# Two attention-and-MLP layers, one token, one core: the last wo loaded behind the last V, and the second layer's next K begun in quarters of chunks

## Chip, core and metric

The kernel runs on one core of a Trainium2 chip. The metric is device time in microseconds, the median of a few runs. Three runs of the kernel before gave 684.42 us (682.33 to 685.11).

## The reference

One token of width 512 goes through attention, MLP, attention, MLP; both attention blocks use the same weights and the same K and V caches, both MLPs the same weights. All of it is float32.

```
def _A_ref(x, k_cache, v_cache, wq, wo):              # 32 heads of 128, 4096 keys
    q = (x @ wq) as heads
    scores = einsum("bhqd,bhkd->bhqk", q, k_cache) * (Dh ** -0.5)
    p = softmax(scores)
    o = einsum("bhqk,bhkd->bhqd", p, v_cache)
    return o @ wo                                     # wq 512x4096, wo 4096x512
def _B_ref(x, w1, b1, w2, b2):                        # width 1376
    return gelu(x @ w1 + b1) @ w2 + b2

x = x + _A_ref(layernorm(x), ...)
x = x + _B_ref(layernorm(x), ...)
x = x + _A_ref(layernorm(x), ...)
x = x + _B_ref(layernorm(x), ...)
```

## The kernel before

**Work.** The 32 heads are taken in eight groups `g` of four. K and V of a group are 8 MiB each (128 partitions by 16384 floats); a group also needs 1 MiB of wq and 1 MiB of wo. K and V come in eight chunks `c` of 1 MiB (NC = 4U columns, U = 512), and a chunk has four quarters of U columns, one for each head. For each group PE computes the queries, the scores against eight chunks of K (`scores`, result in PSUM tile pS), DVE and ACT the softmax (`exponentials`, `weights`), PE the weighted sum of V (`values`, result in pO) and the product with wo (`head_out`). The first layer goes through g = 0 to 7, the second through g = 7 to 0, so that what is still in SBUF at the change of layers is used again.

**Storage.** All large operands live in one SBUF tile, `arena`, cut up by hand. In units of U columns: A is 0 to 32, C 32 to 64, B 64 to 96, of which the last 6 are also the first 6 of SHARED (90 to 100); SCRATCH is 100 (the softmax numerators, and pieces of `head_out` and of the MLP), PAIR is 101 to 109. K and V take A, B and C in turn. `load` (L68) issues one DMA on SyncE's queue (SP). A DMA that overwrites columns must wait until the DMAs that wrote them have landed and the engines that read them are done, and only for the columns that really overlap. SP issues its DMAs strictly in the order in which they are written: one that waits holds up all behind it. PE's matmuls are in the written order too (L74); DVE, ACT and GpSimd are ordered by the framework.

**End of the first layer (L314 to L342).** For g = 7 K is loaded into C in two halves, then wo into PAIR (L321), then V into A in four pieces (L322, 4, 2, 1 and 1 chunks). After the V loop come w1 in four rows (L331, L333) and w2 in four pieces (`load_w2`, called from inside `mlp`), which overwrite one another and SCRATCH in SHARED: the last row of w1 waits for SCRATCH, which `head_out` reads last at L225, and each piece of w2 for the rows of w1 under it.

**Start of the second layer (L346 to L383).** K and V of g = 7 are still in C and A. Of group 6's V 26 quarters were kept in B; six more went to spare PSUM banks (L328) and are copied back by ACT (L375). Group 6's K is loaded anew, by `begin_k`: chunk 0 to SHARED + 4U (over w2 rows 4 to 7), chunk 1 to PAIR + 4U (over the wq used just before), chunks 2 and 3 to C once the scores of g = 7 have read chunk 1 there, chunks 4 to 7 behind them once chunk 5 is read. Then `pair` goes to C + 24U: the wq of the following group (the first 4U) and the wo of group 6 (the other 4U). The two groups are computed from that; `next_queries(2, ...)` at L383 is the last reader of that wq. With n = 2 (group 5) the regular loop begins: K into A, then V into C in two pieces, ((0, 6), (6, 8)), that is C + 0 to 24U and C + 24U to 32U, then the next pair into PAIR, then the next K into B.

**End of the second layer.** As the first, but w1 and w2 go to A, which is free by then (L397 to L400).

Of the kernel before, what the change touches and what calls it, by code (L numbers as in the profile page):

```python
# [28 lines left out]
U = 512  # L29
NC = 4 * U  # L30
# [6 lines left out]
A_AT, B_AT, C_AT = RING  # L37
KEPT_V = 26 * U
SHARED = B_AT + KEPT_V
SCRATCH = SHARED + 10 * U  # L40
PAIR = SHARED + 11 * U
# [9 lines left out]
def decode_layers(ctx: ExitStack, tc: tile.TileContext, x, k, v, w, w1, b1, w2, b2, out):  # L51
    nc = tc.nc
# [4 lines left out]
    def ctile(name, *shape):  # L57
        return const.tile([P, *shape], F32, name=name)
# [6 lines left out]
    def at(first, n):  # L65
        return arena[:, first : first + n]

    def load(first, src):  # L68
        t = at(first, src.shape[-1])
        tc.keep_in_program_order(nc.sync.dma_start(t, src))  # L70
        return t

    def matmul(*a, **kw):
        tc.keep_in_program_order(nc.tensor.matmul(*a, **kw))  # L74

    def quarters(first):
        return [at(first + U * j, U) for j in range(4)]

    def part(src, g, a, b):
        return src[g][:, NC * a : NC * b]  # L80

    def of_w(row, i, n):
        return w[row][:, NC * i : NC * (i + n)]

    def by_four(t):
        return t.rearrange("p (j n) -> p j n", j=4)
# [12 lines left out]
    nc.vector.memset(negmean, -1.0 / D)  # L99
    power = ctile("power", 1)  # L100
    nc.gpsimd.memset(power, -0.5)


    pS, pO = (psum.tile([P, 512], F32, name=n) for n in ("pS", "pO"))
# [34 lines left out]
    def set_x(xin0, scale, xin1, queries=True):  # L139
        s = small("x_sum")  # L140
        t = x_wide if queries else small("x1", 8)
        if not queries:
            nc.gpsimd.memset(pairs(t)[:, :, 1], 1.0)
        x = pairs(t)[:, :, 0]
        nc.vector.scalar_tensor_tensor(x, xin0, scale, xin1, op0=ALU.mult, op1=ALU.add, accum_out=s)  # L145
        if queries:
            for j in range(1, J):
                nc.gpsimd.tensor_copy(pairs(t[:, 32 * j :])[:, :, 0], x)
        return t, s
# [34 lines left out]
    def scores(z, c, kt):  # L184
        for j in range(J):
            matmul(pS[32 * j : 32 * j + C, :], z[:, j, C - 1 - c : 2 * C - 1 - c], kt[j],
                   start=(c == 0), stop=(c == C - 1))

    def exponentials(sc, nsc):
        nc.vector.tensor_reduce(ml[:, 0:1], pS, axis=AX.X, op=ALU.max)  # L190
        mt, m, bias = small("mt", 32), small("m"), small("mt", 32)
        nc.vector.transpose(mt, ml)
        nc.vector.tensor_reduce(m, mt[:, :C], axis=AX.X, op=ALU.max)
        nc.vector.tensor_scalar(mb[:, :C], m.to_broadcast([P, C]), nsc, None, op0=ALU.mult)  # L194
        nc.vector.transpose(bias, mb)  # L195
        p = at(SCRATCH, U)
        nc.scalar.activation(p, pS, AF.Exp, bias=bias[:, 0:1], scale=sc, accum_out=ml[:, 0:1])  # L197
        return p

    def weights(p):  # L200
        for b in range(4):
            tc.keep_in_program_order(nc.tensor.transpose(  # L202
                pT[:, b].rearrange("p j r -> p (j r)"), p[:, P * b : P * (b + 1)], ident))
        pt = work.tile([P, P], F32, name="turned").rearrange("p (j c b) -> p j c b", j=J, c=C)
        nc.vector.tensor_copy(pt, pT[:, :, :, :C].rearrange("p b j c -> p j c b"))  # L205
        lt, l, lr, rl = small("mt", 32), small("l"), small("mt", 32), small("rl")
        nc.vector.transpose(lt, ml)  # L207
        nc.vector.tensor_reduce(l, lt[:, :C], axis=AX.X, op=ALU.add)
        nc.vector.tensor_copy(lb, l.to_broadcast([P, 32]))
        nc.vector.transpose(lr, lb)  # L210
        nc.vector.reciprocal(rl, lr[:, 0:1])
        return pt, rl

    def values(i, pt, vt, c):
        for j in range(J):
            matmul(pO[32 * j : 32 * j + 4, :], pt[:, j, c, :], vt[j],
                   start=(i == 0), stop=(i == C - 1))
# [52 lines left out]
    def load_w1(first, a, b):  # L270
        load(first + W1C * a, w1[:, W1C * a : W1C * b])

    def load_w2(first, a, b):
        load(first + U * a, w2[:, U * a : U * b])
# [4 lines left out]
    def blocks(src, g, home, pieces=((0, C),)):  # L279
        for a, b in pieces:  # L280
            load(home + NC * a, part(src, g, a, b))
            for c in range(a, b):
                yield c, quarters(home + NC * c)

    zero = ctile("zero", 4)
    nc.vector.memset(zero, 0.0)
    xs, s = set_x(zero, 1.0, xcol)

    def first_queries(xs, s, wt):
        for c in range(4):  # L290
            query_block(c, xs, wt)
            if c == 1:
                negm, ss = mean_of(xs, s)
        z = queries(0, negm)
        r = rstd_of(ss)
        sc, nsc = small("sc"), small("nsc")
        nc.vector.tensor_scalar(sc, r, DH ** -0.5, None, op0=ALU.mult)
        nc.vector.tensor_scalar(nsc, r, -(DH ** -0.5), None, op0=ALU.mult)
        return negm, z, sc, nsc
# [6 lines left out]
    def add_up(acc, own):  # L306
        t = small("acc", 4)
        nc.vector.scalar_tensor_tensor(t, own, 1.0, acc, op0=ALU.mult, op1=ALU.add)
        return t


    negm, z, sc, nsc = first_queries(xs, s, wq_t)
    acc = pairs(xs)[:, :, 0]
    for g in range(G):  # L314
        final = g == G - 1
        k_home, v_home = RING[2 * g % 3], RING[(2 * g + 1) % 3]
        for c, t in blocks(k, g, k_home, HALVES if final else ((0, C),)):
            scores(z, c, t)
        pt, rl = weights(exponentials(sc, nsc))
        if final:  # L320
            wo_t = by_four(load(PAIR, of_w(g % 2, g, 1)))  # L321
        for c, t in blocks(v, g, v_home, LAST if final else ((0, C),)):  # L322
            values(c, pt, t, c)
            if g == G - 2:
                for j in range(J):
                    i = 4 * c + j - KEPT_V // U
                    if i >= 0:
                        nc.scalar.copy(pK[i], t[j])  # L328
        if final:
            for i in range(3):  # L330
                load_w1(SHARED, i, i + 1)  # L331
            own = head_out(rl, wo_t, last=True)
            load_w1(SHARED, 3, 4)  # L333
        else:
            pair = load(PAIR, of_w(g % 2, g, 2))
            acc = add_up(acc, head_out(rl, by_four(pair[:, :NC])))
            wq_t = by_four(pair[:, NC:])
            z = next_queries(g + 1, xs, negm, wq_t)
# [4 lines left out]

    g = G - 2  # L346
    negm, z, sc, nsc = first_queries(xs, s, wq_t)
    acc = pairs(xs)[:, :, 0]
    wq_t = by_four(load(SHARED, of_w((g + 1) % 2, g, 1)))
    k_t = []  # L350

    def begin_k(home, a, b):
        load(home, part(k, g, a, b))
        k_t.extend(quarters(home + NC * i) for i in range(b - a))

    begin_k(SHARED + NC, 0, 1)
    begin_k(PAIR + NC, 1, 2)
    for c in range(C):
        scores(z, c, quarters(C_AT + NC * c))
        if c == 1:  # L360
            begin_k(C_AT, 2, 4)
        if c == 5:
            begin_k(C_AT + 2 * NC, 4, 8)
    pair = load(C_AT + 6 * NC, of_w(g % 2, g - 1, 2))
    p = exponentials(sc, nsc)
    z = next_queries(1, xs, negm, wq_t)
    pt, rl = weights(p)
# [2 lines left out]
    acc = add_up(acc, head_out(rl, wo_t))  # L370

    v_t = [at(B_AT + U * i, U) for i in range(KEPT_V // U)]
    for i, first in enumerate([SHARED + 8 * U, SHARED + 9 * U] + [PAIR + U * j for j in range(4)]):
        t = at(first, U)
        nc.scalar.copy(t, pK[i])  # L375
        v_t.append(t)
    for c in range(C):
        scores(z, c, k_t[c])
    pt, rl = weights(exponentials(sc, nsc))
    for c in range(C):  # L380
        values(c, pt, v_t[4 * c : 4 * c + 4], c)
# [1 line left out]
    z = next_queries(2, xs, negm, by_four(pair[:, :NC]))  # L383

    homes = (A_AT, C_AT, B_AT)
    for n in range(2, G):
        g, final = G - 1 - n, n == G - 1
        k_home, v_home = homes[(2 * n - 1) % 3], homes[2 * n % 3]
        for c, t in blocks(k, g, k_home, HALVES if final else ((0, C),)):
            scores(z, c, t)  # L390
        pt, rl = weights(exponentials(sc, nsc))
        if final:
            wo_t = by_four(load(PAIR, of_w(g % 2, g, 1)))
        for c, t in blocks(v, g, v_home, LAST if final else ((0, 6), (6, 8)) if n == 2 else ((0, C),)):
            values(c, pt, t, c)
        if final:
            for a, b in HALVES_W1:  # L397
                load_w1(A_AT, a, b)
            for a, b in W2_AT_END:
                load_w2(A_AT + 11 * U, a, b)  # L400
            own = head_out(rl, wo_t, last=True)
        else:
            pair = load(PAIR, of_w(g % 2, g - 1, 2))
            acc = add_up(acc, head_out(rl, by_four(pair[:, NC:])))
            z = next_queries(n + 1, xs, negm, by_four(pair[:, :NC]))
# [47 lines left out]
```

## Time and profile before

| | |
|---|---|
| median of three runs | 684.42 us (682.33 to 685.11) |
| the profiled execution | 684.1 us, its span 681.9 us, mean granted TensorE clock 0.841 |
| read from HBM | 286.14 MB, 420 GB/s over the span |
| busy: PE, DVE, ACT | 417.0 us (61%), 110.1 us (16%), 22.2 us (3%) |
| who was waited for on PE | DMA in_v 90.3 us, DMA in_k 66.2 us |

The span is the time from the first to the last instruction; the rest of the execution's time lies around it. Positions in the text are microseconds from the span's start. In the rows of the trace, "SPq L70 DMA_DIRECT2D arena<-in_k" is SP issuing a load of K at that moment; when it lands is a separate number, the time to landing.

### The profile page before, as it was taken

The numbers are of one execution on the slowest core, as the hardware profiler recorded it, in microseconds if no ns is written. First come the engines' busy times: TensorE is split into PE (matmuls) and PEld (weight loads), VectorE is DVE, ScalarE is ACT, GpSimd is POOL, SyncE is SP. The second block draws the span as 40 slices with busy tenths as digits, with TensorE's granted clock in tenths as the row PEclk, the third lists the DMA queues.
The fourth block names the chain that finished last, engine by engine and source line by source line (L and its number), as shares of the span: only waits on it lengthen the run. The fifth ranks groups of instructions, "written<-read, shape, count | busy, mean of one in ns | idle before, by whom it ended". The sixth has DMA issues, their size and how long they took to land. (4 is left out here: it accounts for less than half of the span.)

```text
span 681.9 us, 6303 instructions
## 1 busy us (share of the span) xinstructions
PE 417.0 (61%) x2768; PEld 115.8 (17%) x2768; DVE 110.1 (16%) x431; ACT 22.2 (3%) x47; POOL 4.3 (1%) x21
## 2 busy tenths in 40 slices
PE   1536566485564875547656897776456765656755
PEld 0102111021121211112103221221121111211212
DVE  1012101111011111211202212221021101210202
ACT  0010000000000000001000010000000000000000
POOL 1000000000000000000000000000000000000000
PEclk9969878797687876988976898989597876987968
DMA  9999999999999999999999999999999999999996
GB/s 369 432 431 431 439 442 451 432 433 431 428 431 405 454 428 431 431 417 433 430 405 319 354 451 425 399 446 428 443 435 415 455 431 428 431 443 409 428 414 273
DMA packets 10971, 286.54 MB, mean 420 GB/s; under 512 B 1728, under 2 KB 1728, under 8 KB 3008
## 3 DMA queue, kind: packets, MB, share of 16 engines
q1 hardware_dynamic: 10512, 286.14, 98.3%
q8 instruction: 21, 0.34, 0.2%
q10 hardware_dynamic: 432, 0.01, 0.0%
q14 instruction: 6, 0.05, 0.0%
HBM read 286.14 MB, written 0.00 MB: 420 GB/s over the span
## 5 line engine op out<-in xcount | busy, mean ns | idle before, releaser
L74 PE MATMUL pO<-arena,turned 128*4 128x512 f32 x1024 | 143.6, 722 | 91.6 <-DMA arena<-in_v 90.3
L74 PE MATMUL pS<-arena,zq 128*8 128x512 f32 x1024 | 135.1, 687 | 71.9 <-DMA arena<-in_k 66.2
L74 PE MATMUL pO<-arena,x_wide 128*128 128x512 f32 (+1 forms) x176 | 55.7, 533 | 25.1 <-DVE turned L134 18.1
L74 PE MATMUL pO<-arena,on_wide 128*128 128x512 f32 x112 | 51.8, 605 | 18.6 <-DVE on_wide L229 18.6
L74 PEld LDWEIGHTS pO<-arena,turned 128*4 128x4 f32 x1024 | 27.9, 97 | 197.0 <-issue 189.0
L74 PEld LDWEIGHTS pS<-arena,zq 128*8 128x8 f32 x1024 | 28.9, 98 | 174.9 <-issue 165.1
L134 DVE STREAM_TRANSPOSE turned<-pO 32x128 f32<-32x128 f32 x112 | 35.0, 312 | 101.1 <-PE pO L74 99.9
L221 DVE STREAM_TRANSPOSE arena<-pO 128x512 f32<-128x512 f32 x16 | 11.5, 717 | 229.7 <-PE pO L74 229.7
L190 DVE TENSOR_REDUCE ml<-pS 128x1 f32<-128x512 f32 x16 | 11.1, 692 | 183.2 <-PE pS L74 183.2
L202 PE MATMUL pO<-ident,arena 128*128 128x128 f32 x64 | 12.3, 323 | 43.9 <-ACT arena L197 42.4
L74 PEld LDWEIGHTS pO<-arena,x_wide 128*128 128x128 f32 (+1 forms) x176 | 21.8, 160 | 57.8 <-DVE turned L134 26.5
L197 ACT ACTIVATE arena<-pS,mt,sc 128x512 f32<-128x512 f32 x16 | 12.4, 777 | 536.0 <-DVE mt L195 536.0
L74 PEld LDWEIGHTS pO<-arena,on_wide 128*128 128x128 f32 x112 | 20.1, 190 | 51.7 <-DVE on_wide L229 31.6
L202 PEld LDWEIGHTS pO<-ident,arena 128*128 128x128 f32 x64 | 7.9, 159 | 58.5 <-ACT arena L197 51.2
L74 PE MATMUL pS<-arena,gelu_g 128*1 128x128 f32 x176 | 8.1, 329 | 6.8 <-DVE gelu_g L263 4.3
L74 PE MATMUL pO<-arena,x 128*2 128x344 f32 x64 | 7.4, 590 | 1.3 <-DVE x L145 1.3
L74 PEld LDWEIGHTS pS<-arena,gelu_g 128*1 128x1 f32 x176 | 4.3, 94 | 11.2 <-DVE gelu_g L263 5.7
L207 DVE STREAM_TRANSPOSE mt<-ml 128x32 f32<-128x32 f32 x16 | 3.4, 211 | 17.2 <-ACT arena L197 17.2
L74 PE MATMUL pS<-arena,on_wide 128*1 128x128 f32 x64 | 2.9, 344 | 2.6 <-DVE on_wide L227 2.6
L205 DVE COPY turned<-pO 128x128 f32<-128x128 f32 x16 | 4.2, 263 | 1.8 <-PE pO L202 1.8
L242 POOL TENSOR_TENSOR xb<-x,b2c 128x4 f32<-128x4 f32 x2 | 0.4, 198 | 643.3 <-DVE x L145 643.3
L375 ACT COPY arena<-pK 128x512 f32<-128x512 f32 x6 | 3.4, 586 | 20.1 <-issue 13.0
(67 smaller groups left out, 68.6 us busy)
## 6 DMA issues: line engine op xcount, KB each, us to landing
arena<-in_w SPq DMA_DIRECT2D x13, 2048.0 KB, 29.0
arena<-in_k SPq DMA_DIRECT2D x5, 4096.0 KB, 39.2
arena<-in_v SPq DMA_DIRECT2D x2, 4096.0 KB, 19.9
arena<-in_w SPq DMA_DIRECT2D x6, 1024.0 KB, 10.6
arena<-in_v SPq DMA_DIRECT2D x3, 2048.0 KB, 21.2
arena<-in_v SPq DMA_DIRECT2D x1, 6144.0 KB, 26.9
arena<-in_v SPq DMA_DIRECT2D x4, 1024.0 KB, 27.4
arena<-in_w SPq DMA_DIRECT2D x4, 688.0 KB, 30.4
```

Of the source, the lines that this page charges most:

```text
L74: tc.keep_in_program_order(nc.tensor.matmul(*a, **kw))
L134: nc.vector.transpose(t[q], src[q, P * j : P * (j + 1)])
L190: nc.vector.tensor_reduce(ml[:, 0:1], pS, axis=AX.X, op=ALU.max)
L197: nc.scalar.activation(p, pS, AF.Exp, bias=bias[:, 0:1], scale=sc, accum_out=ml[:, 0:1])
L202: tc.keep_in_program_order(nc.tensor.transpose(pT[:, b].rearrange("p j r -> p (j r)"), p[:, P * b : P * (b + 1)], ident))
L205: nc.vector.tensor_copy(pt, pT[:, :, :, :C].rearrange("p b j c -> p j c b"))
L207: nc.vector.transpose(lt, ml)
L221: nc.vector.transpose(ot, pO)
L242: nc.gpsimd.tensor_tensor(xb, pairs(xs)[:, :, 0], b2c, op=ALU.add)
L375: nc.scalar.copy(t, pK[i])
```

## The change

Four edits:

1. At the end of each layer the load of the last wo moves from in front of the four V loads to behind them, in front of w1.
2. `begin_k` loads in quarters instead of chunks, and spreads group 6's K differently: 4 quarters to SHARED + 4U, 2 more to SHARED + 8U (over w2 rows 8 and 9), 4 to PAIR + 4U, 4 to C + 0 once the scores have read chunk 0 there, 4 to C + 4U once chunk 1 is read, and 14 to C + 8U to 22U once chunk 5 is read.
3. `pair` goes to C + 22U (to 30U) instead of C + 24U (to 32U).
4. The first two V quarters that come back from PSUM go to C + 30U and C + 31U instead of SHARED + 8U and 9U.

A memset of a small zero tile also moves to the kernel's start.

```
-    zero = ctile("zero", 4)
-    nc.vector.memset(zero, 0.0)
...
         pt, rl = weights(exponentials(sc, nsc))
-        if final:
-            wo_t = by_four(load(PAIR, of_w(g % 2, g, 1)))
         for c, t in blocks(v, g, v_home, LAST if final else ((0, C),)):
             values(c, pt, t, c)
...
         if final:
+            wo_t = by_four(load(PAIR, of_w(g % 2, g, 1)))
             for i in range(3):
                 load_w1(SHARED, i, i + 1)
...
-    def begin_k(home, a, b):
-        load(home, part(k, g, a, b))
-        k_t.extend(quarters(home + NC * i) for i in range(b - a))
-
-    begin_k(SHARED + NC, 0, 1)
-    begin_k(PAIR + NC, 1, 2)
+    def begin_k(home, n):
+        a = len(k_t)
+        load(home, k[g][:, U * a : U * (a + n)])
+        k_t.extend(at(home + U * i, U) for i in range(n))
+
+    begin_k(SHARED + NC, 4)
+    begin_k(SHARED + 2 * NC, 2)
+    begin_k(PAIR + NC, 4)
     for c in range(C):
         scores(z, c, quarters(C_AT + NC * c))
-        if c == 1:
-            begin_k(C_AT, 2, 4)
+        if c < 2:
+            begin_k(C_AT + NC * c, 4)
         if c == 5:
-            begin_k(C_AT + 2 * NC, 4, 8)
-    pair = load(C_AT + 6 * NC, of_w(g % 2, g - 1, 2))
+            begin_k(C_AT + 2 * NC, 14)
+    pair = load(C_AT + 22 * U, of_w(g % 2, g - 1, 2))
...
-    for i, first in enumerate([SHARED + 8 * U, SHARED + 9 * U] + [PAIR + U * j for j in range(4)]):
+    for i, first in enumerate([C_AT + 30 * U, C_AT + 31 * U] + [PAIR + U * j for j in range(4)]):
...
     for c in range(C):
-        scores(z, c, k_t[c])
+        scores(z, c, k_t[4 * c : 4 * c + 4])
```

The loop of the regular groups, with its `((0, 6), (6, 8))` for n = 2, is not touched but for the place of wo.

The order of instructions moves on SP. At the end of the first layer it is this; the first rows are the second half of K of g = 7, wo, the four pieces of V and two rows of w1, as they stand before:

```order
L70 DMA arena<-in_k 128x8192
L70 DMA arena<-in_w 128x2048 [waits DMAHW0_49,PE_49]
L70 DMA arena<-in_v 128x8192 [waits DMAHW6_49]
L70 DMA arena<-in_v 128x4096
L70 DMA arena<-in_v 128x2048
L70 DMA arena<-in_v 128x2048 [waits DMAHW7_49]
L70 DMA arena<-in_w 128x1376 [waits Activation_49]
```

and of the changed kernel:

```order
L70 DMA arena<-in_k 128x8192
L70 DMA arena<-in_v 128x8192 [waits DMAHW6_49,PE_49]
L70 DMA arena<-in_v 128x4096 [waits PE_49]
L70 DMA arena<-in_v 128x2048 [waits PE_49] x2
L70 DMA arena<-in_w 128x2048 [waits DMAHW7_49,DMAHW0_49,PE_49]
L70 DMA arena<-in_w 128x1376 [waits Activation_49]
```

wo (128x2048) has gone from in front of V to behind it; V waits for PE's scores of group 6 in A instead of standing behind wo's wait.

At the start of the second layer SP holds, before, chunk 1 of group 6's K, the other two loads of that K, `pair`, the K of n = 2, the two pieces of its V, the next pair and the next K. The bracket names the semaphores waited for: DMAHW is a DMA that must have landed, PE and Activation are those engines.

```order
L70 DMA arena<-in_k 128x2048 [waits PE_49]
L70 DMA arena<-in_k 128x4096 [waits PE_49]
L70 DMA arena<-in_k 128x8192 [waits PE_49]
L70 DMA arena<-in_w 128x4096 [waits PE_49]
L70 DMA arena<-in_k 128x16384 [waits PE_49]
L70 DMA arena<-in_v 128x12288 [waits DMAHW4_49,DMAHW7_49,DMAHW3_49,PE_49]
L70 DMA arena<-in_v 128x4096 [waits DMAHW5_49,DMAHW0_49,PE_49]
L70 DMA arena<-in_w 128x4096 [waits DMAHW2_49,DMAHW1_49,Activation_49]
L70 DMA arena<-in_k 128x16384
```

and in the changed kernel, from the two quarters over w2 on:

```order
L70 DMA arena<-in_k 128x1024 [waits DMAHW7_49,PE_49]
L70 DMA arena<-in_k 128x2048 [waits PE_49] x3
L70 DMA arena<-in_k 128x7168 [waits PE_49]
L70 DMA arena<-in_w 128x4096 [waits PE_49]
L70 DMA arena<-in_k 128x16384 [waits DMAHW0_49,PE_49]
L70 DMA arena<-in_v 128x12288 [waits DMAHW5_49,DMAHW6_49,DMAHW4_49,DMAHW7_49,DMAHW1_49,PE_49]
L70 DMA arena<-in_v 128x4096 [waits DMAHW2_49,PE_49,Activation_49]
L70 DMA arena<-in_w 128x4096 [waits DMAHW3_49,Activation_49]
L70 DMA arena<-in_k 128x16384
```

Group 6's K comes in six loads instead of four (the first, of 128x2048, stands in front of these rows in both). The order of what follows is the same; the first piece of V of n = 2 (128x12288) waits for five DMAs instead of three, and its second piece waits for ACT as well.

More of the change, by code (lines that the diff above doesn't have):

```diff
@@ L101, in decode_layers @@
     nc.gpsimd.memset(power, -0.5)
+    zero = ctile("zero", 4)
+    nc.vector.memset(zero, 0.0)
     pS, pO = (psum.tile([P, 512], F32, name=n) for n in ("pS", "pO"))
@@ L391, in decode_layers @@
         pt, rl = weights(exponentials(sc, nsc))
-        if final:
-            wo_t = by_four(load(PAIR, of_w(g % 2, g, 1)))
         for c, t in blocks(v, g, v_home, LAST if final else ((0, 6), (6, 8)) if n == 2 else ((0, C),)):
@@ L396, in decode_layers @@
         if final:
+            wo_t = by_four(load(PAIR, of_w(g % 2, g, 1)))
             for a, b in HALVES_W1:
```

## The prediction

> **What bounds the kernel now.** I read the page's head first, for the engines' and the DMA's shares by slice.
>
> ```profile
> span 681.9 us, 6303 instructions
> PE 417.0 (61%) x2768; PEld 115.8 (17%) x2768; DVE 110.1 (16%) x431; ACT 22.2 (3%) x47; POOL 4.3 (1%) x21
> DMA  9999999999999999999999999999999999999996
> GB/s 369 432 431 431 439 442 451 432 433 431 428 431 405 454 428 431 431 417 433 430 405 319 354 451 425 399 446 428 443 435 415 455 431 428 431 443 409 428 414 273
> ```
>
> No engine is near full; DMA is, nearly all the time, at about 431 GB/s. Its two weak slices besides the last are the 22nd and 23rd, 358 to 392 us: the change of layers, where both large edits lie. So a change counts only if it moves the moment from which DMA is full to the end. Next the busy time by stretches (columns: PE, PEld, DVE, ACT, POOL, PE clock, DMA share, GB/s).
>
> ```profile
> 356.00:366.00 10.00, 5.93 (x88) 1.97 (x80) 3.80 (x18) 0.21 (x1) 0.75 (x2) 0.83 0.81 272
> 366.00:376.00 10.00, 7.02 (x136) 3.80 (x136) 1.48 (x10) 1.07 (x2) 0.48 (x4) 0.53 0.98 368
> 376.00:390.00 14.00, 12.70 (x72) 3.19 (x72) 3.69 (x18) 0.87 (x2) 0.50 (x1) 0.85 0.89 336
> 390.00:412.00 22.00, 18.36 (x140) 5.12 (x140) 4.64 (x16) 2.34 (x4) 0.00 (x0) 1.00 1.03 443
> 412.00:434.00 22.00, 16.80 (x84) 5.16 (x84) 4.54 (x18) 0.87 (x2) 0.00 (x0) 0.92 1.00 433
> 438.00:674.00 236.00, 147.90 (x924) 39.73 (x916) 38.70 (x146) 5.21 (x12) 0.75 (x2) 0.83 1.00 431
> ```
>
> Against 431 GB/s the first three rows lose 159, 63 and 95 GB/s over 10, 10 and 14 us, 3.55 MB or **8.2 us**: all that the change could win. Behind 390 DMA is full to 674, but for some 0.8 us around 434. The chain of work that ended last shows who leads in between (start, length, what):
>
> ```profile
> 391.36 7.09 PE pO L74 x64
> 403.43 7.03 PE pS L74 x64
> 414.22 8.79 PE pO L74 x64
> 429.37 3.71 PE pO L74 x8
> 434.72 7.10 PE pS L74 x64
> 464.64 46.49 DMA arena<-in_k
> 654.77 22.97 DMA arena<-in_w
> 677.78 0.62 PE pS L74 x16
> ```
>
> From 391 to 442 it is PE that works without waiting for data (values and scores of g = 7 and 6, then `next_queries(2)` at 429.37), while DMA fills buffers as PE frees them; later K and V are waited for again, a load queueing 46 us. So in this stretch the kernel lives on loads that can be issued well ahead of PE.
>
> **Edits 2 to 4: where V of n = 2 may land.** The SP rows of this stretch:
>
> ```profile
> 385.29 0.33 SPq L70 DMA_DIRECT2D arena<-in_w  x1
> 398.47 0.33 SPq L70 DMA_DIRECT2D arena<-in_k  x1
> 410.48 22.96 SPq L70 DMA_DIRECT2D arena<-in_v  x2
> 433.57 0.34 SPq L70 DMA_DIRECT2D arena<-in_w  x1
> 433.95 0.43 SPq L70 DMA_DIRECT2D arena<-in_k  x1
> ```
>
> and, in the same order, what the DMA view gives for their size and time to landing (the second of V's two pieces left out):
>
> ```profile
> arena<-in_w SPq DMA_DIRECT2D x1, 2048.0 KB, 18.2
> arena<-in_k SPq DMA_DIRECT2D x1, 24.4
> arena<-in_v SPq DMA_DIRECT2D x1, 6144.0 KB, 26.9
> arena<-in_w SPq DMA_DIRECT2D x1, 2048.0 KB, 14.6
> arena<-in_k SPq DMA_DIRECT2D x1, 33.5
> ```
>
> Before, V's first piece, chunks 0 to 5 into C + 0 to 24U, needs only group 6's scores, which end at 410.46 (403.43 + 7.03). It is issued at 410.48, while K of n = 2 still flows (398.47 + 24.4 = 422.87), and DMA goes on without a gap. Its second piece lies over `pair` and waits for `next_queries(2)`, 429.37 + 3.71 = 433.1.
>
> With `pair` at C + 22U to 30U, its first two U, chunks 0 and 1 of the wq for `next_queries(2)`, lie **inside** the first piece's 0 to 24U, and the split ((0, 6), (6, 8)) was not moved along. The first piece, too, must now wait until PE has multiplied with these two chunks, half of the eight matmuls from 429.37: 429.37 + 1.85 = 431.2 on the old clock of events, less what PE gains earlier. The order rows bear it out: that load now waits for five DMAs, and four have written into C + 0 to 24U (at C + 0, + 4U, + 8U, and `pair`), and the fifth is the last use of its own semaphore. Behind it on SP stand V's second piece, the next pair and the next K, which waited until 433 anyway, so nothing else is held up; but DMA has nothing to do from K's landing on.
>
> *How much earlier PE gets there.* The path runs from the last V of g = 7 through MLP and first queries:
>
> ```profile
> 352.34 1.78 PE L74 MATMUL pO<-arena,turned 128*4 128x512 f32 x12
> 355.57 1.04 PE L74 MATMUL pO<-arena,turned 128*4 128x512 f32 x8 [1.45 <-DMA arena<-in_v]
> 357.67 0.33 SPq L70 DMA_DIRECT2D arena<-in_w  x1
> 371.31 1.46 PE L74 MATMUL pS<-arena,gelu_g 128*1 128x128 f32 x24 [0.38 <-DMA arena<-in_w]
> 376.15 9.07 PE L74 MATMUL pS<-arena,zq 128*8 128x512 f32 x64 [0.71 <-DVE pS L168]
> arena<-in_w SPq DMA_DIRECT2D x1, 1024.0 KB, 5.1
> ```
>
> Edit 1 puts 1 MiB of wo behind V, so the last V lands one such transfer earlier, 2.4 us (1.05 MB at 431 GB/s), at about 353.1. The last row of w1, issued at 357.67 once SCRATCH was free, goes out as much earlier, and the hole of 356 to 366 closes: from 353.1 on wo, w1 (2.8 MB) and w2 (2.9 MB) flow one after the other, 6.75 MB. At 431 GB/s they have landed at 368.8 instead of shortly before 371.31, 2.5 us earlier; with w2's 2.9 MB at the 368 GB/s of the row for 366 to 376, 1.4 us earlier. wo itself lands where V did, when `head_out` wants it. I take **2.2 us**, nearer to the full rate, as the queue is never empty there; the ends go into the range. Behind that all is PE, DVE and ACT, so first queries, both groups and `next_queries(2)` come 2.2 us earlier: V's first piece is issued at **429.0**.
>
> ACT's copies to C + 30U and 31U now wait for the first scores (end 376.15 + 9.07 = 385.2) and stand in front of the exponentials on ACT:
>
> ```profile
> 372.03 1.07 ACT L375 COPY arena<-pK 128x512 f32<-128x512 f32 x2 [6.26 <-PE pS L74]
> 387.04 0.78 ACT L197 ACTIVATE arena<-pS,mt,sc 128x512 f32<-128x512 f32 x1 [13.94 <-DVE mt L195]
> ```
>
> The exponentials began 1.8 us after the scores, for which DVE's maximum works; two copies take 1.07 of that: hidden, 0.7 us to spare.
>
> *What it costs.* From an idle queue the kernel's first load, 1 MiB, took 5.1 us to land, 2.7 more than its 2.4 of transfer. Then V, pair and the next K, 18.87 MB, take 43.8 us at 431 GB/s: that K lands at 429.0 + 2.7 + 43.8 = 475.5. Before it landed at 433.95 + 33.5 = 467.45. **+8.0 us.** Everything the edits win in filling the hole (group 6's K and `pair` landing up to 8 us earlier, K of n = 2 up to 4) ends in an idle stretch: K of n = 2 can be issued when the values free A, 398.47 - 2.2, and has landed by 396.3 + 2.7 + 19.5 = 418.5, after which DMA waits some 13 us. From 431 on DMA is full in both kernels, and the whole difference goes to the end.
>
> [...]
>
> **Edit 1 at the second layer's end.** V lands 2.4 us earlier, wo where V's last piece did, w1 and w2 as before. The chain's last rows are 22.97 us of in_w and the 16 matmuls behind it: the end waits for the last of w2, whose place in the queue is the same. 0 us; if wo were late there it would be at most its 2.4 us, hidden under 5.7 MB (13 us) of w1 and w2. The moved memset runs while the first load is under way: 0.
>
> **Sum.** The profiled execution took 684.1 us (2.2 around its span), within 0.3 us of the median 684.42. 684.1 + 8.0 = **692.1 us**.
>
> **The rivals.**
>
> *PE gains nothing (694.3).* If w1 and w2, which are waited for piece by piece, keep their old pace (the hole only moves), V's first piece goes out at 431.2: +10.2. For it: PE waits 0.38 us for w2 at the very end of it. Against: the last w1 row is released by V alone.
>
> *PE gains two more (690.1).* The scores from 376.15 took 9.07 us, those from 434.72 7.10, because the granted clock was 0.53 in 366 to 376. With full clock the issue comes 2 us earlier still: +6.0. For it: shorter waits for w2. Against: they remain. [...]
>
> *The other side: V is not held (679.6).* If the first piece were still released by group 6's scores, at 410.48 - 2.2, no gap would open. K of n = 2 would then begin at 396.3 + 2.7 = 399.0, against 403.5 before (385.29 + 18.2, the landing of `pair` in front of it): 4.5 us faster, 679.6. It is decided by whether 22U to 24U is read after those scores. By the addresses it is, and only a `pair` from 24U on would avoid it.
>
> *No change.* PE would have to reach `next_queries(2)` by about 421, 10 us earlier; 9.07 + 7.09 + 7.03 + 8.79 us of matmuls lie between, at a clock of 0.85 or more. Almost excluded.
>
> **How the numbers follow.** Forecast 64%, PE gains nothing 15%, PE gains two more 14%, V not held 3%, near no change 4%. Range 689.0 to 695.5: from the second rival less about 1 to the first plus about 1 for the restart's price and the runs' spread. A measurement of this kernel can tell about 0.5% (3.4 us) from no change: slower by more 93%, within it 4%, faster 3%.
>
> **What would show it.** In the changed profile: V's first piece issued at about 429 rather than 408, in the middle of `next_queries(2)`; DMA near full from 353 to 395 and a new hole of 11 to 15 us from about 418; the last V of layer one at 353 and the last w2 near 369; the K behind V landing near 475; the end of both kernels alike but for the shift. I am wrong if that load is issued at 408, or if DMA has work in the hole.

## The result and the profile after

| | before | after |
|---|---|---|
| median | 684.33 us of 5 (682.21 to 685.11) | **694.0 us** of 5 (692.94 to 696.31) |
| ratio | | **1.0151** (95%: 1.0123 to 1.018) |
| profiled execution, its span | 684.1, 681.9 us | 696.3, 694.4 us |

1.5% slower, 9.7 us by the medians; the profiled execution of the changed kernel is the longest of its five, 12.2 us over that of before. First the head of its page: the span, the busy share of the DMA engines in 40 slices of 17.4 us, and what they moved.

```profile
span 694.4 us, 6310 instructions
DMA  9999999999999999999999992999999999999996
GB/s 412 431 423 419 428 427 446 445 420 427 431 430 435 445 420 427 438 416 427 424 344 333 424 454 106 399 460 428 423 446 438 424 430 429 428 443 415 428 418 264
```

The 25th slice, 417 to 434 us, is new: a 2 among nines, 106 GB/s. The two weak slices of before, the 21st and 22nd here, are still there. The same stretches as in the prediction (columns as there: the last three are PE clock, DMA share, GB/s):

```profile
356.00:366.00 10.00, 6.02 (x96) 2.05 (x96) 2.78 (x16) 0.21 (x1) 0.75 (x2) 0.81 0.84 284
366.00:376.00 10.00, 6.05 (x112) 3.21 (x114) 0.93 (x7) 0.00 (x0) 0.43 (x3) 0.53 0.93 358
376.00:390.00 14.00, 12.60 (x88) 3.39 (x80) 3.80 (x19) 1.94 (x4) 0.55 (x1) 0.85 0.94 358
...
412.00:434.00 22.00, 16.64 (x84) 4.92 (x84) 4.64 (x19) 0.87 (x2) 0.00 (x0) 0.92 0.45 179
...
438.00:674.00 236.00, 144.97 (x840) 37.92 (x832) 35.41 (x131) 5.21 (x12) 0.00 (x0) 0.80 1.00 430
```

412 to 434 fell from 433 GB/s to 179: 254 GB/s over 22 us, 5.6 MB or 13 us at 431 GB/s. Ahead of it the change won little in this trace: against 431 the first three rows lose 147, 73 and 73 GB/s, 3.2 MB or 7.5 us, where before lost 8.2. The DMA view of 396 to 444 in slices of 1.2 us shows the hole's edges:

```profile
DMA  8999959393909191919100000000009192997996
GB/s 382 423 437 806 437 218 655 164 710 123 765 0 819 55 819 55 819 55 819 55 0 0 0 0 0 0 0 0 0 0 614 41 532 123 621 382 328 573 410 287
```

(Nine and one by turns still is a full queue: 819 and 55 average 437.) From 420 to 432 nothing moves at all. SP's rows of this stretch, what the DMA view gives for V's first piece, and the chain of waits:

```profile
371.86 12.47 SPq L70 DMA_DIRECT2D arena<-in_k  x6
...
398.92 0.33 SPq L70 DMA_DIRECT2D arena<-in_k  x1
431.69 2.10 SPq L70 DMA_DIRECT2D arena<-in_v  x2
...
434.34 0.47 SPq L70 DMA_DIRECT2D arena<-in_k  x1
```

```profile
arena<-in_v SPq DMA_DIRECT2D x1, 6144.0 KB, 18.3
```

```profile
429.67 3.71 PE pO L74 x8
...
433.46 0.33 SPq L70
...
434.34 44.77 DMA arena<-in_k
479.11 0.14 issue
479.24 8.78 PE pS L74 x64
```

V's first piece went out at 431.69, not at 410.48, 2.0 us into the eight matmuls of `next_queries(2)` from 429.67. SP stood at it from 398.92 on, and everything written behind it waited too. The chain now runs through `next_queries(2)` and SP into the K behind V, which landed at 479.11 (434.34 + 44.77) instead of 467.45: 11.7 us of the 12.2.

### The profile page after: what moved, and what is told of

Same layout as the page of the kernel before. It is cut to its first block, busy times and chain, and to the rows that moved or that the text cites. A ratio compares the mean times of both kernels' runs of the same rounds, so it can differ in the third digit from the quotient of the medians.

```text
span 694.4 us, 6310 instructions
## 1 busy us (share of the span) xinstructions
PE 423.5 (61%) x2768; PEld 117.1 (17%) x2768; DVE 110.4 (16%) x431; ACT 22.2 (3%) x47; POOL 4.3 (1%) x21
## 5 line engine op out<-in xcount | busy, mean ns | idle before, releaser
L74 PE MATMUL pO<-arena,turned 128*4 128x512 f32 x1024 | 146.4, 733 | 88.2 <-DMA arena<-in_v 87.4
L74 PE MATMUL pS<-arena,zq 128*8 128x512 f32 x1024 | 136.6, 693 | 77.9 <-DMA arena<-in_k 72.2
## 6 DMA issues: line engine op xcount, KB each, us to landing
arena<-in_v SPq DMA_DIRECT2D x1, 6144.0 KB, 18.3
```

## The experiments

Theory H, on record in the prediction: the whole slowdown is V's first piece, held by the wq in C + 22U and 23U, and edit 1 and the quarters are worth a little or nothing. Its rivals: the quarters themselves (more, smaller loads) or the moved wo cost the time. The kernels ran on three chips, where the kernel before had medians of 683.98 us (19 runs), 684.02 (29) and 684.67 (28); each ratio is to before on the same chip. No kernel leaves out any of the work.

### The wait alone, in the kernel before

```
-LAST if final else ((0, 6), (6, 8)) if n == 2
+LAST if final else ((0, 7), (7, 8)) if n == 2
```

> The kernel before, with one number changed: V of n = 2 comes in pieces of 7 and 1 chunks instead of 6 and 2, so that its first piece lies over the whole wq that next_queries(2) still has to read. Nothing of the change is in it. My theory (the wait of that piece for next_queries(2) is what costs): the piece is issued at about 433 instead of 410, DMA idles from about 423 to 436, and the time is 433.1 + 3 + 43.8 - 467.4 = 12 us above before, 696 us. Rival (the slowdown comes from something else in the change: the smaller loads of K, the moved wo, ACT's copies): the wait is hidden and this kernel stays at 684.4.

Measured: 697.88 us, ratio 1.0208 (1.0182 to 1.0233). `pair` lies at C + 24U here, as in the kernel before, and the first piece, now 0 to 28U, lies over it. The SP rows, and V's time to landing:

```profile
434.23 0.81 SPq L70 DMA_DIRECT2D arena<-in_v  x2
...
435.55 0.71 SPq L70 DMA_DIRECT2D arena<-in_k  x1
```

```profile
arena<-in_v SPq DMA_DIRECT2D x1, 7168.0 KB, 20.5
```

One number makes the same hole (191 GB/s in 412 to 434) in a kernel with neither quarters nor moved wo. It is later than in the changed kernel since the piece waits for the whole wq in `pair`, not for half of it.

### The changed kernel without the wait

```
-LAST if final else ((0, 6), (6, 8)) if n == 2
+LAST if final else ((0, 5), (5, 8)) if n == 2
```

> The changed kernel with V of n = 2 in pieces of 5 and 3 chunks: its first piece (C + 0 to 20U) no longer touches wq at C + 22U. My theory: the first piece is issued behind group 6's scores, at about 411; its 5 MiB last until about 434, the second piece can go at 433.5 and begins about 436, so a hole of 2 us is left instead of 11; the time is 685 (684 to 687), within 0.5% of before. Rival (the slowdown comes from the smaller loads or from wo): it stays at 692 to 694.

Measured: 683.77 us, ratio 1.0003 (0.9984 to 1.0023). The first piece, 0 to 20U, no longer touches `pair`. Its SP rows, and what DMA moved in slices of 1.2 us from 396 on:

```profile
409.24 23.09 SPq L70 DMA_DIRECT2D arena<-in_v  x2
...
432.85 0.43 SPq L70 DMA_DIRECT2D arena<-in_k  x1
```

```profile
GB/s 437 546 696 55 710 164 710 109 669 218 655 218 655 218 608 273 601 218 471 171 512 444 512 512 205 478 478 512 171 68 205 123 471 471 362 471 430 328 430 423
```

The whole slowdown is gone by one number, so neither the quarters nor the moved wo cost it. But nothing is won either. The slices say why: only 5 MiB of V, not 6, can flow ahead of `next_queries(2)`, and they run out. In the 29th to 32nd slice (171, 68, 205, 123), 429.6 to 434.4, DMA moves 142 GB/s, which is 3.2 us lost against 431, about as much as this kernel's DMA gains ahead of it, from 356 to 390 (363 GB/s on average, before 327: 2.8 us).

### Each half of the change alone

Edits 2 to 4, with wo back in front of V at both ends:

```
+        if final:
+            wo_t = by_four(load(PAIR, of_w(g % 2, g, 1)))
         for c, t in blocks(v, g, v_home, ...
...
         if final:
-            wo_t = by_four(load(PAIR, of_w(g % 2, g, 1)))
```

> The changed kernel without edit 1 (wo in front of V again), so edits 2 to 4 alone. My theory: V's first piece waits for next_queries(2) as in the changed kernel, at 431 to 432, and the time is 694 (692 to 696), so edits 2 to 4 hold the whole slowdown. If edit 1 did bring PE forward in the changed kernel, this one is up to 2 us slower than the changed kernel. Rival (the moved wo does the harm): back at 684.

Measured: 694.8 us, ratio 1.0159 (1.0131 to 1.0187), as much as the whole change. Its SP row, V's landing and the chain:

```profile
430.05 2.46 SPq L70 DMA_DIRECT2D arena<-in_v  x2
```

```profile
arena<-in_v SPq DMA_DIRECT2D x1, 6144.0 KB, 18.3
```

```profile
433.06 44.46 DMA arena<-in_k
```

Edit 1 alone, in the kernel before (the same diff the other way round):

> The kernel before with edit 1 alone (wo behind V at the end of both layers). By the step of my prediction, PE reaches the second layer 2.2 us earlier and, as DMA is behind from there on, the whole kernel gains about that: 682.2. By the rival that PE gains nothing, which the changed kernel's trace speaks for (V's first piece at 431.7 instead of 429.0): 684.4, no difference beyond 1 us. In no theory is it slower than 686.

Measured: 683.31 us, ratio 0.9994 (0.9974 to 1.0014): no difference that can be told. Edit 1 for the second layer's end alone, since the changed kernel's trace showed 0.9 us more behind the last w2 there (below):

> The kernel before with edit 1 at the second layer's end alone. My prediction put 0 us on it. The traces so far speak against: with wo behind V, PE's MLP waits for w1 with its clock halved and multiplies w2 (88 matmuls) in 4.1 to 4.9 us without waiting for data, and the output went out 1.9 to 3.4 us after w2 had landed instead of 1.1. If edit 1 costs at the end, this kernel is 0.9 to 2 us slower than before, 685 to 686, with such a tail in its trace. If the clock falls that way or the other whatever stands there (without edit 1 two of four traces had such a tail too), it is within 0.5 us: 684.

Measured: 684.51 us, ratio 1.0003 (0.9983 to 1.0022). The prediction's 0 us for that edit stands in the times.

### How much earlier PE gets to `next_queries(2)`

The prediction had edit 1 bring PE there 2.2 us earlier. In the changed kernel it came at 429.67, before at 429.37. The PE rows of its change of layers:

```profile
343.17 6.78 PE L74 MATMUL pO<-arena,turned 128*4 128x512 f32 x48 [3.42 <-DMA arena<-in_v]
350.47 1.04 PE L74 MATMUL pO<-arena,turned 128*4 128x512 f32 x8 [0.52 <-DMA arena<-in_v]
352.95 1.89 PE L74 MATMUL pO<-arena,turned 128*4 128x512 f32 x8 [1.44 <-DMA arena<-in_v]
356.16 1.88 PE L74 MATMUL pS<-arena,on_wide 128*1 128x128 f32 x32 [1.32 <-DVE on_wide L230]
...
368.47 1.46 PE L74 MATMUL pS<-arena,gelu_g 128*1 128x128 f32 x24 [2.87 <-DMA arena<-in_w]
...
372.22 1.46 PE L74 MATMUL pS<-arena,gelu_g 128*1 128x128 f32 x24 [0.43 <-DMA arena<-in_w]
...
377.06 8.62 PE L74 MATMUL pS<-arena,zq 128*8 128x512 f32 x64 [0.71 <-DVE pS L171]
```

The last V is there at 352.9, as predicted (353.1; before 355.6). But the same eight matmuls take 1.89 us and not 1.04: the granted clock is 0.50 here, from 352.96 to 359.79 (before 1.00, from 349.6 to 359.7), and `head_out`'s 32 take 1.88 instead of 1.05, as this row of before has them:

```profile
357.93 1.05 PE L74 MATMUL pS<-arena,on_wide 128*1 128x128 f32 x32 [1.32 <-DVE on_wide L227]
```

That spends 1.7 us of the 2.2; then PE waits 2.87 us for the second piece of w2, and the last comes at 372.2 instead of 371.3. SP's row that begins with w1's last row in the changed kernel, and the time to landing of w2's three pieces of 768 KB, in the changed kernel and before:

```profile
355.90 13.99 SPq L70 DMA_DIRECT2D arena<-in_w  x6
```

```profile
arena<-in_w SPq DMA_DIRECT2D x3, 768.0 KB, 8.3
arena<-in_w SPq DMA_DIRECT2D x3, 768.0 KB, 6.1
```

w1's last row goes out 1.8 us earlier than before (357.67), but it now queues behind wo and the other rows of w1 and lands at 362.0, only 0.7 us earlier (6.1 us after issue, before 5.1). The last piece of w2 lies over that row and goes out when PE and DVE are done with it, at 363.81 (before 364.86). In this trace it then takes 8.4 us to land and not 6.4: of the 16 marks that its landing leaves in the trace 14 stand by 370.5, the last two at 371.3 and 372.2.

The other kernels show the same order. In the eight with wo behind V in layer one, w1's last row goes out at 354.9 to 356.0 and lands at 362.0 to 362.4, and the last piece of w2 goes out at 363.8 to 364.7 and lands at 369.7 to 372.2. In the five with wo in front it is 357.4 to 358.0, 361.9 to 363.2, 363.7 to 365.9 and 369.9 to 372.3. By the means PE has the last of w2 0.8 us earlier, not the 1.4 to 2.5 of the prediction. The halved clock is not needed for it: with edit 1 alone the clock is full up to 362.9 (1.00 in 357.4 to 360.8, 0.81 in 360.8 to 364.2), and the last piece goes out at 363.83 all the same.

To see whether the halved clock is what holds PE up, matmuls with columns of zeros (into pS, whose scores have been read by then, so they only keep PE busy) fill its waits for the last pieces of V:

```
+    def keep_busy(n):
+        for i in range(n):
+            j = i % J
+            matmul(pS[32 * j : 32 * j + 7, :], zq[0][:, j, C : 2 * C - 1], at(C_AT + U * j, U), start=True, stop=True)
...
         for c, t in blocks(v, g, v_home, LAST if final else ((0, C),)):
+            if final:
+                keep_busy({0: 6, 6: 2, 7: 5}.get(c, 0))
             values(c, pt, t, c)
```

> The changed kernel with 13 matmuls by a block of zeros (into pS, overwritten later) in PE's waits for the last V pieces of layer one: 6 ahead of the first, 2 ahead of the third, 5 ahead of the last. They take nothing that is needed and keep PE busy. In the changed kernel's trace PE's clock was halved from 353.0 to 359.8, and head_out's matmuls took 1.88 us instead of 1.05. If that is why PE did not gain its 2.2 us: clock 1.0 there, head_out and MLP about 1.5 us earlier, V's first piece at about 430 instead of 431.7, and the time 1 to 2 us under the changed kernel: 692. If w2's landing alone sets PE's pace: clock better, V's piece and the time as they were, 694.

Measured: 694.25 us, ratio 1.0158 (1.0116 to 1.02). Two stretches of its trace, with the columns as above, and SP's row for V:

```profile
354.00:357.40 3.40, 1.14 (x33) 0.77 (x33) 1.61 (x6) 0.00 (x0) 0.20 (x1) 1.00 1.02 408
357.40:360.80 3.40, 2.86 (x36) 1.16 (x40) 0.66 (x6) 0.00 (x0) 0.09 (x1) 0.52 0.86 309
```

```profile
428.77 2.10 SPq L70 DMA_DIRECT2D arena<-in_v  x2
```

The clock stays full to 357 (1.00) and is halved after it instead (0.52). V goes out at 428.77, where the prediction had it, and 2.9 us earlier than in the changed kernel's trace; but the median, 694.25, is that of the changed kernel, 694.0 (ratios 1.0158 and 1.0151). One execution's gain of that size is within what executions of one kernel differ by; that the filling wins anything is not shown.

Over all kernels the start of `next_queries(2)` in their one profiled execution was 429.37, 428.04, 430.50, 428.96 and 426.65 where wo is loaded in front of the last V of layer one, and 429.67, 425.53, 428.21, 424.54, 426.76, 427.94, 429.49 and 428.10 where it is loaded behind (426.76 and 427.94 with the filling): means of 428.7 and 427.5. If edit 1 wins anything there it is about 1.2 us, with 4 to 5 us between executions.

### What the filling is worth when V is not held

`pair` back to C + 24U, the two V quarters to C + 22U and 23U, and V of n = 2 in three pieces, so that one piece lies under the copies and one under `pair`:

```
-    pair = load(C_AT + 22 * U, of_w(g % 2, g - 1, 2))
+    pair = load(C_AT + 24 * U, of_w(g % 2, g - 1, 2))
...
-enumerate([C_AT + 30 * U, C_AT + 31 * U] + ...
+enumerate([C_AT + 22 * U, C_AT + 23 * U] + ...
...
-((0, 6), (6, 8)) if n == 2
+((0, 5), (5, 6), (6, 8)) if n == 2
```

> The changed kernel with the wait taken apart: pair back at C + 24U, the two V quarters from PSUM at C + 22U and 23U, and V of n = 2 in pieces of 5, 1 and 2 chunks. The first piece needs only group 6's scores, the second the values of group 6 (about 422), the third next_queries(2) (about 432), each before DMA is done with the one ahead. My theory: no idle stretch from 420 to 436 at all; K of n = 2 lands at 421.5 (422.9 before) and the K behind V at 465 (467.5 before); 682 us, 2 us under before. Rival (the filled hole is worth the 4.5 us of my prediction's other side): 679.6. Rival (it gains nothing, as the split into 5 and 3 chunks did): 684.

Measured: 682.43 us, ratio 0.9973 (0.9953 to 0.9994). Its SP rows and the stretch:

```profile
405.68 22.92 SPq L70 DMA_DIRECT2D arena<-in_v  x3
...
429.12 0.42 SPq L70 DMA_DIRECT2D arena<-in_k  x1
```

```profile
412.00:434.00 22.00, 17.64 (x112) 5.20 (x108) 4.02 (x13) 0.00 (x0) 0.00 (x0) 0.98 0.96 410
```

The hole is closed, and the K behind V lands at 464.1 (429.12 + 35.0), 3.3 us earlier than before. The profiled execution is only 1.0 us shorter, 683.07 to 684.1: 2.4 us are given back at the very end (next). Two variations of it, without edit 1:

> The same without edit 1 (wo in front of V): edits 2 to 4 alone, without their wait. If edit 1 brings PE forward, this is 1 to 2 us slower than the one with it: 683 to 684. If PE's gain is only scatter of the clock and of w2's landing, both are the same within 1 us.

Measured: 683.78 us, ratio 0.9987 (0.9963 to 1.001), which can't be told from the version with edit 1 nor from before. And with the 13 filling matmuls:

> The kernel with pieces of 5, 1 and 2 chunks and the same 13 filling matmuls. If the clock is what held PE back: 1 us under the kernel without them, 681. Otherwise the same time.

Measured: 682.64 us, ratio 0.9982 (0.9963 to 1.0001): again the filling at the first layer's end shows no gain.

### The end of the second layer

The last matmuls of the second layer's MLP, before, and then in the changed kernel:

```profile
674.97 1.06 PE L74 MATMUL pS<-arena,gelu_g 128*1 128x128 f32 x32 [2.20 <-DVE gelu_g L263]
676.53 1.06 PE L74 MATMUL pS<-arena,gelu_g 128*1 128x128 f32 x32 [0.51 <-DMA arena<-in_w]
677.78 1.04 PE L74 MATMUL pS<-arena,gelu_g 128*1 128x128 f32 x24 [0.19 <-DMA arena<-in_w]
```

```profile
683.34 1.67 PE L74 MATMUL pO<-arena,x 128*2 128x344 f32 x16 [0.61 <-DMA arena<-in_w]
687.22 4.25 PE L74 MATMUL pS<-arena,gelu_g 128*1 128x128 f32 x88 [2.21 <-DVE gelu_g L266]
```

Before, PE takes the 88 matmuls in three runs of about 1.05, the second and the third waiting for their piece of w2, and ends 0.4 us behind the landing of the last. In the changed kernel the granted clock over the 88 is 0.60 (before 1.00, from 674.97 to 678.82), they take 4.25 us in one run without waiting for a piece, and the output goes out 1.96 us behind the landing of the last piece (690.12), where before it was 1.05 (678.38): 0.9 more. In the seven profiled kernels with edit 1 at that end these 1.96 are 1.9 to 3.4 (in the three-piece version the 88 take 4.87 us), but three of the five without it and without filling have 1.8 to 2.2 as well. Edit 1 at the first layer's end alone, on the three-piece version:

> The kernel with pieces of 5, 1 and 2 chunks and edit 1 at the first layer's end only. If edit 1 costs 1 to 2 us at the second end: 681, under the kernel with both (682.4). If not: the same, 682 to 683.

Measured: 681.65 us, ratio 0.9956 (0.9937 to 0.9975). It ran on another chip than the version with edit 1 at both ends (0.9973, 0.9953 to 0.9994), and the intervals overlap: that edit 1 costs something at the second end is not shown. The same with seven filling matmuls at the second layer's end, 3 ahead of `head_out`'s and 4 ahead of w2's:

```
                 load_w2(c)
+        if not load_w2:
+            keep_busy(4)
...
                 load_w2(A_AT + 11 * U, a, b)
+            keep_busy(3)
             own = head_out(rl, wo_t, last=True)
```

> The same with seven matmuls by a block of zeros into pS at the second layer's end (3 ahead of head_out's, 4 ahead of w2's), to keep PE busy there. If the halved clock makes the tail: w2's 88 matmuls run at full clock as they land, the output leaves about 1.1 us after the last landing, and the kernel is 0 to 1.5 us under the one without them. If not: the same or 0.5 us slower.

Measured: **680.81 us, ratio 0.995 (0.993 to 0.997)**, the fastest version here. Its last matmuls:

```profile
672.25 1.05 PE L74 MATMUL pS<-arena,gelu_g 128*1 128x128 f32 x32 [1.35 <-DVE gelu_g L273]
673.66 1.05 PE L74 MATMUL pS<-arena,gelu_g 128*1 128x128 f32 x32 [0.36 <-DMA arena<-in_w]
674.88 1.03 PE L74 MATMUL pS<-arena,gelu_g 128*1 128x128 f32 x24 [0.17 <-DMA arena<-in_w]
```

Three runs of 1.03 to 1.05 us, as before at a granted clock of 1.00, and the end as short as before. That the filling did it is not shown: before and the kernel with pieces of 7 and 1 have the same short end (1.05 us) without any. The ratios of the two versions, 0.9956 and 0.995, have intervals that overlap, so its worth is not measured apart.

## Why the prediction was right, and which terms were off

**What bounds the kernel: right.** From 438 to 674 DMA runs at 431 GB/s before and at 430 in the changed kernel. With V held, what was lost in the hole came out at the end one for one. Four kernels give it (issue of V's first piece; landing of the K behind it; profiled time): 428.77, 476.43, 693.97 with filling; 430.05, 477.52, 694.62 without edit 1; 431.69, 479.11, 696.31 for the changed kernel; 434.23, 481.77, 698.49 for the kernel before with the other split. The middle differences are 47.66, 47.47, 47.42 and 47.54 us, the last ones between 216.7 and 217.5, before's 216.65.

**V's first piece waits for half of `next_queries(2)`: right, and shown both ways** (one number puts the hole into the kernel before, one number takes it out of the changed one). "V not held" and "no change" fell with it.

**PE 2.2 us earlier: this is the step that failed.** The prediction had w1 and w2 flow "one after the other" behind V, "as the queue is never empty there". The row of 356 to 366 has 284 GB/s, hardly more than before's 272. w1 lands where the sum puts it (353.1 and 3.85 MB at 431 GB/s make 362.0), but w2 is not in the queue behind it by then: each piece goes out only when the rows of w1 under it have been read, the last at 363.81, and w1's last row lands at 361.9 to 363.2 in every kernel, wo in front or behind. V's piece went out at 431.69 instead of 429.0, **+2.7 us**, in the trace the rival "PE gains nothing"; the halved clock and the late end of w2's landing have a part in that, in this one trace. Over all traces edit 1 looks worth 1.2 us, within their scatter; the size is open. The median, 694.0, is nearer to that rival's 694.3 than to the forecast's 692.1; with the 0.9 us of the next term added to both (695.2 and 693.0) it lies in between.

**Restart 2.7 us: a size that was off.** V's 6.29 MB take 14.6 us at 431 GB/s and landed 18.3 after issue: 3.7. The same comes from the middle differences, 47.4 to 47.7 less 43.8: 3.6 to 3.9. **+0.9** in the trace of the changed kernel (47.4 against the 46.5 of the sum). The traces with V held agree: its first piece took 17.7 to 18.3 us for 6 MiB in three of them and 20.5 for 7 MiB in the fourth, 3.1 to 3.7 more than its transfer at 431 GB/s.

**Second layer's end at 0 us: right in the times** (1.0003 for that edit alone), though the changed kernel's trace has **+0.9** there, with the granted clock at 0.60 over w2's matmuls.

The sum in the trace: 8.0 + 2.7 + 0.9 + 0.9 = 12.5, the difference of the spans (694.4 and 681.9). The median, 9.7 us over before, is less far off, since that execution is the longest of the five. The three misses all point the same way, and the 696.3 of that execution lies above the range; the median is inside it.

**ACT's copies: hidden, as predicted.**

```profile
385.81 1.07 ACT L378 COPY arena<-pK 128x512 f32<-128x512 f32 x2 [21.09 <-PE pS L74]
387.49 0.78 ACT L200 ACTIVATE arena<-pS,mt,sc 128x512 f32<-128x512 f32 x1 [0.61 <-DVE mt L198]
```

They end 0.6 us before the exponentials can begin, which still wait for DVE.

**Where the aim of the change went.** Of the 8.2 us that DMA loses at the change of layers the changed kernel's trace wins back 0.7, and it is the weakest: from 356 to 390 it has 336 GB/s on average, while the ten kernels with the quarters or with edit 1 at the first layer's end have 336 to 377, 363 in the mean, and the three with neither 314 to 332, 324 in the mean. That is about 3.1 us won, an estimate from a fixed stretch of the traces, and the wait of V's first piece swallows it. Smaller loads start when their room is free, and the room comes free at the pace of PE: the six loads of group 6's K go out between 371.9 and 384.3. With V not held the best version is 3.9 us faster by the medians (680.81 and 684.67), not 8.2.

## What to carry to other kernels

When a buffer is moved within a shared tile, list every later load whose rectangle touches its new place and its old one, and ask when the last reader of each is done: an overlap of 2U in a load of 24U held up all of it for 21 us. Split a large load at the borders of what lies under it, so that one late reader holds only its own piece: with V in three pieces and `pair` back at C + 24U DMA moved 410 GB/s from 412 to 434 instead of 179, and the median was 682.43 us instead of 694.0. DMA was full here from 438 to 674 (431 GB/s before, 430 in the changed kernel), and the moment when V's first piece went out set the time one for one: in the four kernels with V held, which issued it up to 5.5 us apart, the K behind it landed 47.4 to 47.7 us later and the profiled time was 216.7 to 217.5 us past that. A gap filled ahead of it, worth an estimated 3.1 us here, showed in the time only where that load could follow at once.

## What the hardware showed beside that

The clock was halved without a long idle stretch of PE. In the changed kernel's trace the granted clock is 1.00 from 346.2 to 352.9 and 0.50 from 352.96 to 359.79; in the 3.0 us ahead of the halving, from 349.95 to 352.95, PE worked 1.04 us, and its longest idle there was 1.44. With edit 1 alone PE's rows are nearly the same there (1.04 us of work in the 3.06 from 349.89 to 352.95, idle for 0.58 and 1.44), and the granted clock stays at 1.00 from 350.6 to 360.8. So these 3 us of PE's work do not settle by themselves when the clock is halved; what does is not shown.

Between the 13 profiled executions, each of another kernel, the start of `next_queries(2)` differs by up to 6 us (424.5 to 430.5) and the time from the last load to the output by up to 2.4 (1.05 to 3.4); the clock has a part in both (the eight matmuls with the last V took 1.04 us at a granted clock of 1.00 and 1.89 at 0.50, the 88 with w2 3.13 us of PE at 1.00 and 4.25 at 0.60), and an edit worth 1 or 2 us can't be read from a single trace.

From an idle queue DMA did not only start late: in the 12 us from 432 on the slices of the changed kernel average 391 GB/s against 431, some 1.1 us of transfer (0.48 MB), about what the restart's price was underestimated by; that it is the same 0.9 us is not shown. The other three kernels with V held have 388 to 394 GB/s in the 12 us that begin 0.3 us after the issue.
